# Loading the first batch of an attention kernel in token halves, with values sorted on TensorE

## The chip, the cores and the metric

The kernel runs on one core of a Trainium2 chip. The metric is device time in microseconds (us). Kernels of one set of experiments were timed on one chip, in rounds with runs of the kernel before on it, and are compared with those. The sets ran on different chips, on which the kernel before had medians of 236.9 to 237.4 us. Each run was checked for a slower state of the chip; none showed it.

## The reference

Four batches of 768 tokens with 8 heads of 64. Tokens attend in chunks of 32 to their chunk, 16 tokens to its left, 8 to its right and 8 memory tokens. The result, 512 wide, passes a layer to 2048 wide with a snake activation and a layer back to 512.

```python
for c in range(S // 32):                       # attention by chunks
    k_full = concat([mem_k, k[l_start:r_end]])
    a = softmax(q_c @ k_full.T / sqrt(64))
    out[c] = a @ concat([mem_v, v[l_start:r_end]])
h = x @ w_in                                   # x: 3072 x 512
s = sin(alpha * h)
g = h + s * s / (alpha + 1e-9)
return g @ w_out
```

## The kernel before

Batches run one behind the other. Of each, 8 blocks of 96 queries go through attention; then 16 tiles of the first layer (L1), with the second layer of the batch before it streamed between as filler. The change touches the opening, where batch 0 has nothing to hide behind. A piece is the k or q of two heads. Its heads are copied side by side (paired, tile pr), turned by six matmuls on TensorE (transposed, tile tt) and copied out of PSUM, the memory that matmuls write to, into kTi or qT (evicted). Filler matmuls (tile z) work on zeros and only keep TensorE busy. In the views PE is TensorE, DVE is VectorE, ACT is ScalarE and POOL is GpSimd, which also issues most of the loads (DMA).

```python
def spin(n):                        # filler matmuls on zeros
    z = smp.tile([P, 512], F32, name="z", tag="sm")
    for _ in range(n):
        nc.tensor.matmul(z[:], zeros[:, 0:P], zeros[:])
# ... 8 loads: k and q of two heads each, 128 partitions x 6 tokens
for hp in range(1, HP):
    load_qk_pair(0, hp, *kq)
# ... values: 2 loads a block, one token per descriptor
for j in range(NJ):
    load_v(0, j)
nc.sync.dma_start(alpha_sb[:], moe_alpha.rearrange("(ft p) -> p ft", p=P))
# ... a piece: pair two heads, transpose 6 x 128, evict
for n in range(2 * HP):
    (t_k if n % 2 == 0 else t_q)(prs[n], n // 2)
    spin(2)
# ... then, per block: scores and exponentials (sc, pt), values
# (ot, rinv, x_blk), transposes back (xtp, xT)
xT = burst(0, stream, (), 2)
# ... L1: u = sin, s = square, gT = h + s / alpha; the string says
# which engine squares each tile (A ScalarE, D VectorE, P GpSimd)
sq = ("ADADADAAADADADAA" if i == 0 else "ADAAPDADADAPADAD")[ft]
if 1 <= ft:
    stream.take(3 if last else 2)   # second-layer matmuls as filler
```

The softmax here doesn't subtract the row's maximum and nothing guards it: scores larger than these inputs give would overflow.

## Time and profile before

| | before |
|---|---|
| time, median of its first 3 runs | 237.71 us (237.04 to 239.23) |
| profiled span, mean granted clock | 234.8 us, 1.000 |
| first exponential | 17.06 us |
| last copy to xT (attention of batch 0 done) | 29.26 us |
| first sine (L1 of batch 0 begins) | 30.65 us |
| last gT of batch 0 | 55.09 us |
| first sine of batch 3 to the end | 51.12 us |

Times of events are counted from the start of the profiled span. The page, the chain and the groups are shown in the prediction.

### The profile page before, as it was taken

Reading aid. Unit: us, or ns where it says so; the run is one execution under the profiler, and the core shown is the slowest. Engines: PE = TensorE matmul, PEld = TensorE weight load, DVE = VectorE, ACT = ScalarE, POOL = GpSimd, SP = SyncE. Lnnn points to the kernel's source line nnn. Section 1 sums busy time; section 2 is a strip of 40 time slices with the busy share of each in tenths; the row PEclk is TensorE's granted clock in tenths of the full one; section 3 lists DMA queues with packets and bytes.
Section 4 is the critical chain, followed back from the end, with each engine's and each line's share of the span. In section 5 each row is a group of like instructions: output and inputs, shape, how many; then the busy total and the mean of one; then the engine's idle time right before and its main releaser. Section 6 shows DMA issues by size and latency. Waiting matters only on the chain.

```text
span 234.8 us, 4467 instructions
## 1 busy us (share of the span) xinstructions
PE 217.1 (92%) x1759; PEld 122.3 (52%) x1785; DVE 160.8 (69%) x287; ACT 153.8 (66%) x237; POOL 72.1 (31%) x96
## 2 busy tenths in 40 slices
PE   7588799979989999998999999998999999899994
PEld 2355565545545556664455556564555555453453
DVE  3596969999338877988557598978466358875110
ACT  3489679984794397899664787779564676880000
POOL 7899855214832115139120115120000020010000
PEclk9999999999999999999999999999999999999999
DMA  7999999999999910019999101001111110101122
GB/s 78 160 141 82 141 187 204 206 207 157 142 218 160 153 48 3 0 46 133 181 150 113 47 0 45 3 0 45 47 45 47 46 45 3 45 0 45 59 78 89
DMA packets 53852, 21.11 MB, mean 90 GB/s; under 512 B 36296, under 2 KB 50888, under 8 KB 53832
## 3 DMA queue, kind: packets, MB, share of 16 engines
q0 software_dynamic: 47616, 14.40, 72.4%
q1 hardware_dynamic: 6216, 6.43, 9.4%
q8 instruction: 14, 0.23, 0.4%
q14 instruction: 6, 0.05, 0.1%
HBM read 28.91 MB, written 6.29 MB: 150 GB/s over the span
## 4 chain that ended last, share of the span: by engine, by line
PE 60%; DVE 15%; ACT 11%; issue 7%; DMA 3%; POOL 2%; POOLq 1%; DVEq 0%; ACTq 0%
PE o L398 29%; PE hT L341 19%; DVE gT L370 6%; ACT pt L275 4%; ACT u L353 3%; DMA q_bf<-in_q_dram 3%; PE ot L288 3%; DVE s L362 3%; PE sc L266 3%; ACT s L356 2%; PE ot L306 2%; DVE x_blk L293 2%; PE o L387 1%; PE tt_a L257 1%; PE tt_a L242 1%
## 5 line engine op out<-in xcount | busy, mean ns | idle before, releaser
L398 PE MATMUL o<-w_out_sb,gT 128*128 128x512 bf16 x343 | 93.1, 380 | 2.0 <-issue 0.5
L341 PE MATMUL hT<-xT,w_in_sb 128*128 128x384 bf16 x488 | 87.3, 326 | 3.8 <-DVE gT L370 3.4
L370 DVE SCALAR_TENSOR_TENSOR gT<-s,inv_alpha,hT 128x768 bf16<-128x768 f32 x61 | 60.8, 1012 | 21.6 <-ACT s L356 13.7
L353 ACT ACTIVATE u<-hT,alpha_sb 128x768 f32<-128x768 f32 x61 | 54.7, 898 | 25.5 <-PE hT L341 24.4
L341 PEld LDWEIGHTS <-w_in_sb 128*128 128x128 bf16 x512 | 49.3, 98 | 38.5 <-issue 4.7
L275 ACT ACTIVATE pt<-sc,biasm 128x256 bf16<-128x256 f32 x96 | 37.6, 493 | 12.5 <-PE sc L266 12.4
L398 PEld LDWEIGHTS <-gT 128*128 128x128 bf16 x368 | 31.9, 98 | 26.1 <-DVE gT L370 1.2
L358 POOL TENSOR_TENSOR s<-u 128x768 f32<-128x768 f32 x6 | 8.8, 1466 | 71.6 <-ACT u L353 61.3
L356 ACT ACTIVATE s<-u 128x768 f32<-128x768 f32 x34 | 28.7, 843 | 1.1
L362 DVE TENSOR_TENSOR s<-u 128x768 f32<-128x768 f32 x24 | 24.9, 1036 | 0.6 <-ACT u L353 0.5
L293 DVE TENSOR_TENSOR x_blk<-ot,rinv 96x512 bf16<-96x512 f32 x32 | 22.0, 686 | 1.1
L226 POOL COPY pr<-q_bf 128x768 bf16<-128x768 bf16 x12 | 10.1, 839 | 38.6 <-PE tt_a L242 23.7
L292 DVE RECIPROCAL rinv<-ot 96x8 f32<-96x8 f32 x32 | 6.5, 202 | 20.1 <-PE ot L288 19.6
L407 ACT COPY o_sb<-o 128x512 f32<-128x512 f32 x11 | 6.4, 585 | 20.0 <-PE o L398 20.0
L405 DVE COPY o_sb<-o 128x512 f32<-128x512 f32 x12 | 8.2, 687 | 15.4 <-PE o L398 15.1
L288 PEld LDWEIGHTS <-pt 128*128 128x128 bf16 x256 | 11.9, 98 | 7.3 <-issue 2.3
L171 PE MATMUL z<-zeros 128*128 128x512 bf16 x36 | 13.2, 451 | 1.3 <-DVE zeros L165 1.3
L288 PE MATMUL ot<-vw,pt 128*128 128x65 bf16 x256 | 13.0, 193 | 0.9 <-ACT pt L275 0.6
L266 PEld LDWEIGHTS <-kTi 64*128 64x128 bf16 x256 | 7.0, 94 | 13.2 <-issue 6.7
L266 PE MATMUL sc<-qT,kTi 64*128 64x96 bf16 x256 | 11.4, 205 | 2.1 <-ACT pt L275 1.2
L306 PEld LDWEIGHTS <-x_blk 96*128 96x128 bf16 x128 | 8.4, 97 | 6.6 <-DVE x_blk L293 1.6
L226 POOL COPY pr<-k_bf 128x768 bf16<-128x768 bf16 x8 | 6.6, 826 | 11.2 <-PE tt_a L257 5.8
(66 smaller groups left out, 180.6 us busy)
## 6 DMA issues: line engine op xcount, KB each, us to landing
out_dram<-o_sb SPq DMA_DIRECT2D x23, 256.0 KB, 2.5
k_bf<-in_k_dram POOLq DMA_DIRECT2D x3, 768.0 KB, 9.1
q_bf<-in_q_dram POOLq DMA_DIRECT2D x3, 768.0 KB, 12.9
vw<-in_v_dram POOLq DMA_DIRECT2D x6, 384.0 KB, 17.7
w_in_sb<-in_moe_w_in_dram POOLq DMA_DIRECT2D x8, 256.0 KB, 9.0
w_out_sb<-in_moe_w_out_dram POOLq DMA_DIRECT2D x4, 512.0 KB, 18.5
k_bf<-in_k_dram POOLq DMA_DIRECT2D x4, 192.0 KB, 6.1
q_bf<-in_q_dram POOLq DMA_DIRECT2D x4, 192.0 KB, 6.7
```

The lines of the kernel that those rows point to most:

```text
L171: nc.tensor.matmul(z[:], zeros[:, 0:P], zeros[:])
L226: (eng or nc.gpsimd.tensor_copy)(pr[:].rearrange("p r e d -> p e r d"), src[:, 2 * hp:2 * hp + 2])
L266: nc.tensor.matmul(sc[:, e, QW * hp:QW * hp + QW], kTi[64 * e:64 * e + 64, hp, 104 * j:104 * j + P], qT[64 * e:64 * e + 64, hp, QW * j:QW ...
L275: nc.scalar.activation(pt[:, 0:H * QW].rearrange("p (g e c) -> p e g c", g=4, e=2)[:, :, :, 32 * m:32 * m + 32], sc[:, :, 0:4 * QW].rearra ...
L288: nc.tensor.matmul(otv[:, h // 4, h % 4, :], pt[:, QW * h:QW * h + P], vws[b % 2][:, h, j, 0:D + 1])
L293: nc.vector.tensor_tensor(out=x_blk[:].rearrange("p (g e) d -> p g e d", g=2), in0=otv[0:QW, :, :, 0:D], in1=rv.unsqueeze(3).to_broadcast( ...
L341: nc.tensor.matmul(hts[hf][:, 0:HALF], w_in_sb[:, kt, P * ft:P * ft + P], xT[:, kt, HALF * hf:HALF * hf + HALF], start=(kt == 0), stop=(kt ...
L353: nc.scalar.activation(u[:], hT[:, :, 0:HALF], ACTF.Sin, scale=alpha_sb[:, ft:ft + 1])
L356: nc.scalar.activation(s2[:], u[:], ACTF.Square)
L362: nc.vector.tensor_tensor(out=s2[:], in0=u[:], in1=u[:], op=ALU.mult)
L370: nc.vector.scalar_tensor_tensor(out=gv, in0=s2[:], scalar=inv_alpha[:, ft:ft + 1], in1=hT[:, :, 0:HALF], op0=ALU.mult, op1=ALU.add)
L398: nc.tensor.matmul(o[:], gT[:, ft, P * s:P * s + P], w_out_sb[:, ft, :], start=(ft == 0), stop=(ft == FT - 1),)
```

## The change

The intent is an earlier start and more overlap in the opening. The first k and q loads bring what the first four query blocks need (576 of the 768 tokens of k, 384 of q). Those blocks may begin while the second halves still load, and one hand-written order mixes the rest in. Values of blocks 0 to 3 are loaded two tokens per descriptor, which halves the number of descriptors. They arrive in the wrong rows, so 4 matmuls with a selection matrix put each pair of blocks in order. A few smaller edits ride along: fewer fillers after the pieces, larger weight loads, half of the first L1 tile begun early, another square string, and fewer second-layer matmuls per tile in the last batch.

```diff
-    for hp in range(1, HP):
-        load_qk_pair(0, hp, *kq)
+    load_qk_part(0, k, kq[0], 0, 0, 96)      # 4 heads, partitions 0:96
+    load_qk_part(0, q, kq[1], 0, 0, 64)
+    load_qk_part(0, k, kq[0], 4, 0, 96)
+    load_qk_part(0, q, kq[1], 4, 0, 64)
...
-    for j in range(NJ):
-        load_v(0, j)
+    for j in range(4):
+        load_v_pairs(j)                      # 2 tokens per descriptor
+    load_qk_part(0, k, kq[0], 0, 96, P)      # second halves
... (three more second halves, then load_v for blocks 4 to 7)
+    def put_v(i, eng):                       # sort two blocks
+        ps = big.tile([P, 2, 512], F32, name="vp", tag="big")
+        for e in range(2):
+            for c in range(2):
+                nc.tensor.matmul(ps[:, c], sel[64 * c:64 * c + 60, e],
+                    v2[64 * c:64 * c + 60, i, :, D * e:D * e + D],
+                    start=(e == 0), stop=(e == 1))
+        eng(vws[0][...], ps[...])
+        put_memv_part(2 * i, 2)
...
-        spin(2)                              # after each first piece
+        spin(1)
...
-    xT = burst(0, stream, (), 2)
+    for word in (  # Q scores, V sort, P values, X xT, R pair, T transpose,
+                   # Z filler, W/N loads, M memory values, E early L1 half
+        "M0 Q0 Z1 Q1 Z1 V0 Q2 P0 V1 Q3 Z1 X0 R8 R9 P1 T8 R10 T9 R11 W0 W1 X1 Z1 T10 T11 R12 R13 Z1 T12 "
+        "R14 T13 R15 W2 W3 W4 Z1 T14 T15 N0 Z1 Q4 P2 Z1 Q5 Q6 P3 X2 P4 Q7 X3 P5 X4 P6 X5 P7 E0 X6 X7"
+    ).split():
+        at(word[0], int(word[1:]))
...
-            sq = ("ADADADAAADADADAA" if i == 0 else ...)[ft]
+            sq = ("ADADAAPADPADPAPA" if i == 0 else ...)[ft]
-                stream.take(3 if last else 2)
+                stream.take(2)
```

## The prediction

> **What bounds the kernel now.** I read, in this order, the page, the chain that ended last (part 4, then in order of time), the groups of instructions of the opening stretch, VectorE's timeline, and the landing of each early load. The change rewrites only the opening (batch 0), so the first question is what sets the end of the opening.
>
> From the page, busy tenths of 40 slices of 5.87 us:
>
> ```profile
> PE   7588799979989999998999999998999999899994
> ...
> DVE  3596969999338877988557598978466358875110
> ACT  3489679984794397899664787779564676880000
> POOL 7899855214832115139120115120000020010000
> ...
> DMA  7999999999999910019999101001111110101122
> ```
>
> TensorE is the bound of the whole (92%), but it is full only from about slice 5 on. In slices 0 to 4 (0 to 29 us) much of its work is filler matmuls on zeros (36 of them, 13.2 us in the groups). So what counts is when the first layer of batch 0 starts; all that follows is a chain behind it.
>
> The chain in order of time, 0 to 60 us (start, length, what):
>
> ```profile
> 5.66 6.97 DMA q_bf<-in_q_dram
> 12.64 0.02 issue
> 12.66 0.46 DVE pr L226
> 13.12 0.61 DVE kTi L243
> ...
> 17.06 5.59 ACT pt L275 x15
> ...
> 24.47 0.69 DVE x_blk L293
> 25.16 0.27 DVE xT L309
> 25.42 0.13 DVE rinv L292
> ...
> 28.90 0.37 DVE xT L309
> 29.27 0.04 issue
> 29.32 1.31 PE hT L341 x7
> 30.63 0.02 issue
> 30.65 0.91 ACT u L353
> ```
>
> It reads as three legs. To 12.7 us the loads of k and q; to 17.06 the pairing, transposing and evicting; then exponentials and, from about 22 us, VectorE alone, which repeats reciprocal, scaling and copy at 1.1 us a block (0.13 + 0.69 + 0.27). The first sine starts at 30.65 us. The reader should note who has room: in 5.5 to 29.3 us the stretch view gives VectorE 17.8 us busy of 23.8, so only 6.0 idle, and most of that is early: 4.7 us waiting for k and q to land, 1.9 for the first values' matmuls.
>
> The groups that price the change, 5.5 to 29.3 us:
>
> ```profile
> L293 DVE TENSOR_TENSOR x_blk<-ot,rinv 96x512 bf16<-96x512 f32 x8 | 5.5, 686 | 0.3
> L243 DVE COPY kTi<-tt_b 128x672 bf16<-128x672 bf16 x3 | 2.6, 851 | 0.8 <-PE tt_b L242 0.8
> L226 DVE COPY pr<-k_bf 128x768 bf16<-128x768 bf16 x4 | 1.9, 464 | 4.2 <-DMA k_bf<-in_k_dram 4.2
> ```
>
> [...]the early loads share one stream: issued 0.7 us apart (1.32, 2.26, 3.52, 4.24, 4.95, 5.66, 6.37, 7.08), they land one after another at 5.6, 7.7, 8.9, 10.7, 11.7, 12.7, 13.7 and 14.6 us. [...]672 bf16 elements out of PSUM take 851 ns, 768 within SBUF as little as 359. This prices the sorted values, which come out of PSUM in fp32. [...]a value load whose issue takes 0.75 us elsewhere took 1.37 us at 16.38 us, beside the 8x4096 copy of VectorE (16.24 to 17.47), and the pair copies spread from 359 to 623 ns while GpSimd issued loads. So I price new pair copies at 0.42 us, not at their best.
>
> **The change, part by part.**
>
> Loads. First k is now 96 rows of 4 heads (1.5 of the old loads), first q 64 rows of 4 heads (1 load), then the same again: five old loads in place of eight. Interpolated in the landings above: 6.6, 8.3, 10.7 and 11.7 us. The last needed before the first scores comes 2.9 us sooner than 14.6.
>
> Values. The first four blocks are 4 loads in place of 8, so GpSimd saves 4 issues of 0.7 us, and w_in is 5 loads in place of 8; the weights come some 5 us sooner. No wait on w_in stands in the chain of before, so this alone buys nothing.
>
> To the first exponential. VectorE must, in its own order after 10.7 us: pair k (0.42), two small memory copies (0.22 + 0.20), evict the second k piece, pair, evict, pair a q, evict. A k piece of 480 columns scales from 851 ns to about 0.57, with one 48-column copy 0.13: 0.70. Sum 0.42 + 0.42 + 0.70 + 0.42 + 0.70 + 0.42 + 0.70 = 3.8, so 14.5; the last q piece and the score matmuls make the first exponential 15.1. That is 2 us before 17.06.
>
> From there VectorE owes, in pitch rather than length: reciprocal 0.2; the cast of memory values, moved here from ScalarE (2048 elements, estimate 1.2); memory rows into the values 1.3; one eviction of sorted values (1024 fp32 from PSUM; 512 take 0.67 in the output copy, so 1.2); eight second-half pair copies, 8 x 0.42 = 3.4; four second-half k evictions of 192 and 48 columns, 4 x 0.4 = 1.6; eight blocks at 1.1 = 8.8. Sum 17.7, so 32.2 if it never waits. Before, the same stretch held the memory rows, a reciprocal and the blocks: about 10.5 us in 12.2. Against the whole stretch the change adds about 5.9 us of VectorE work to an engine that had 6.0 idle, and some 4 us of that idle (the wait for the first load's successors, the tail) cannot be filled.
>
> Waits inside: the build's order shows the copy of memory rows behind ScalarE's eviction of the second pair of blocks (about 0.9), block 2's values behind the last transposes and scores (about 1.1), and the first sorted values behind their matmuls (0.5). Some hide; I take 1.8. So the last xT copy ends at about 34.0, against 29.26. The first half of tile 0 of the first layer is then already done, so the sine follows after 4 matmuls (0.65) instead of 8: 34.8 against 30.65, a **loss of 4.1 us**.
>
> First layer of batch 0. Squares go from 10 ScalarE, 6 VectorE to 8, 4 and 4 on GpSimd. From 30.65 to 55.10 VectorE is busy 21.7 and ScalarE 22.4 of 24.45; TensorE needs 128 x 0.163 = 20.9. ScalarE saves 2 x 0.75 = 1.5, VectorE 2 x 0.9 = 1.8; but a GpSimd square takes 1.47 us and holds its PSUM tile longer, and three such tiles rotate. I take **0.9 us gained** of 1.5.
>
> Last batch. Two filler matmuls a tile instead of three spread what is left of the layer before over more tiles. TensorE idles 0.88, 0.27, 0.38 us and less around 204 to 214 us, where the filler has run out. I take **0.8 gained**.
>
> Sum: +4.1 - 0.9 - 0.8 = +2.4 us. My waits are hand-made and the order looks tuned, so I shade the loss to 1.3: 237.7 + 1.3 = 239.0.
>
> **Rivals.** First, the loads are the whole story: the start moves by 2 to 3 us and the rest hides in ScalarE's and TensorE's room; then about 234. For it: the chain's first leg is a load (6.97 us). Against it: VectorE's 1.1 us cadence from 22 us on, with no idle to take the extra copies. Second, VectorE waits more than I think, since half-pieces, values and blocks all pass it in one fixed order, and the transposes share two PSUM slots; xT then ends at 36 and the time is 242. Third, VectorE's pair copies run at 0.36 [...], and waits hide: xT at 32, time 236.5. A TensorE bound does not arise: the added transposes and the 8 sorting matmuls take under 5 us of time in which it now spins on zeros.
>
> **Range and chances.** From 236 (third rival with both gains in full) to 242 (second): I give 235.5 to 242.3. 2% is 4.75 us. Faster than 233.0 would need the first rival at its best: 0.04. Slower than 242.5 needs the second and no gains: 0.09. Same: 0.87.
>
> **What would show it.** First exponential near 15 us; VectorE almost without idle from 14 us to the last xT copy, which ends at 32 to 36; first sine near 34.8; pair copies of 64 rows still about 0.4 us; sorted-value copy about 1.2; first layer about 23.5 us from its first sine to its last gT; less TensorE idle in the last first layer. It is wrong if the first sine comes at or before 31 us, which means VectorE had room that I did not see, or if weights turn out to be waited for.

## More of the kernel before

One view more is needed here. It gives the busy time of each engine over one stretch, with the number of instructions in brackets, the granted TensorE clock and the busy share of the data-transfer engines. The stretch is from the end of the last k eviction to the last xT, in the kernel before:

```profile
core 0: us, PE busy (x) PEld busy (x) DVE busy (x) ACT busy (x) POOL busy (x), PEclk, DMA share, GB/s
16.24:29.26 13.02, 10.74 (x173) 6.84 (x173) 10.47 (x27) 10.66 (x26) 12.48 (x17) 1.00 1.24 108
```

VectorE (DVE) is busy for 10.47 of 13.02 us, so it waits 2.5 us. The clock is full (1.00).

## The result, and the profile after

The changed kernel took 249.23 us (median of 4 runs, 247.83 to 249.85), against 237.38 us (237.04 to 239.23) for the kernel before in the same rounds. The ratio is 1.0474, with a 95% interval of 1.0403 to 1.0545: slower. A ratio here is the mean time of one kernel's fast runs over that of the other's of the same rounds, so it is not quite the ratio of the medians.

| us | before | after | difference |
|---|---|---|---|
| first exponential | 17.06 | 18.12 | +1.06 |
| last xT | 29.26 | 42.63 | +13.37 |
| first sine, batch 0 | 30.65 | 43.53 | +12.88 |
| L1 of batch 0, first sine to last gT | 24.44 | 25.85 | +1.41 |
| last gT of batch 0 to first sine of batch 3 | 128.57 | 128.13 | -0.44 |
| first sine of batch 3 to the end | 51.12 | 50.06 | -1.06 |
| profiled span | 234.78 | 247.57 | +12.79 |

The whole loss lies before the first sine. Part 2 of the page of the changed kernel, in 40 slices of 6.19 us:

```profile
PE   5497798997899899999899999999999999999994
DVE  4375849779892687889865769898756468867101
PEclk9655556999999999999999999999999999999999
```

TensorE (PE) has holes in its first slices (4 in the second, 7 in the fourth and fifth), and its granted clock is half (5) from 7.4 to 41.6 us; before, it was full from 6.4 us on. The same stretch as above, last first-half k eviction to last xT, now reads:

```profile
16.90:42.63 25.73, 21.34 (x232) 13.27 (x230) 17.85 (x48) 14.01 (x31) 15.63 (x18) 0.52 1.28 159
```

VectorE has 17.85 us of work, where the prediction had 17.7, but it takes 25.73 us over it. It waits 7.9 us where the prediction gave 1.8. The view of waits for VectorE in this stretch names them (what waited, for what: total, times, longest):

```profile
DVE rinv L368 <- PE ot L364: 3.4, 3, 1.7
DVE vw L332 <- PE vp L327: 1.4, 1, 1.4
DVE kTi L299 <- PE tt_a L296: 1.2, 3, 0.5
DVE vw L160 <- ACT vw L332: 1.1, 1, 1.1
```

The second and fourth are the sorting: VectorE waits for the sorting matmuls, and later behind ScalarE's eviction of the second pair. The first is the output of the values, late because TensorE is late. The chain that ended last, in order of time, shows why (start, length, what):

```profile
3.41 8.19 DMA k_bf<-in_k_dram
11.73 0.35 DVE pr L255
...
12.27 0.59 PE z L184
12.85 0.43 PE tt_b L314 x6
13.28 0.54 PE z L184
13.82 0.48 PE tt_b L296 x6
...
19.53 0.98 PE vp L327 x4
20.54 1.24 DVE vw L332
21.80 0.43 DVE vw L160
...
22.37 0.60 PE ot L364 x8
22.97 0.99 PE vp L327 x4
23.98 1.02 ACT vw L332
25.02 0.42 DVE vw L160
```

The second load of first-half k lands at 11.6 us (issued at 3.41, 8.19 us), 0.9 later than predicted. From 12.3 to 20.5 us the chain is TensorE alone, a filler (z) in turn with a group of six transposes, and from 17.6 us with scores and sorting. Before, the chain of that time was a load, then the last piece on VectorE, TensorE and ScalarE, then exponentials. Then follows a relay: sorting, eviction, memory rows, values, sorting again. Each engine waits for the one before it.

### The profile page after: what moved, and what is told of

Same layout as the page of the kernel before. It is cut to its first block, busy times and chain, and to the rows that moved or that the text cites. A ratio compares the mean times of both kernels' runs of the same rounds, so it can differ in the third digit from the quotient of the medians.

```text
span 247.6 us, 4604 instructions
## 1 busy us (share of the span) xinstructions
PE 227.9 (92%) x1830; PEld 128.2 (52%) x1830; DVE 166.1 (67%) x307; ACT 153.0 (62%) x240; POOL 71.6 (29%) x91
## 4 chain that ended last, share of the span: by engine, by line
PE 67%; DVE 11%; ACT 8%; issue 7%; DMA 3%; POOL 2%; POOLq 1%; DVEq 0%; ACTq 0%
PE o L483 28%; PE hT L420 20%; DVE gT L455 5%; PE ot L364 4%; PE sc L342 4%; DMA k_bf<-in_k_dram 3%; ACT u L438 3%; PE z L184 3%; DVE s L447 2%; ACT pt L351 2%; POOL s L443 2%; PE ot L382 2%; PE o L472 1%; ACT s L441 1%; PE tt_a L286 1%
## 5 line engine op out<-in xcount | busy, mean ns | idle before, releaser
L483 PE MATMUL o<-w_out_sb,gT 128*128 128x512 bf16 x368 | 99.0, 380 | 0.6 <-DVE gT L455 0.4
L443 POOL TENSOR_TENSOR s<-u 128x768 f32<-128x768 f32 x10 | 14.7, 1470 | 91.1 <-ACT u L438 80.8
L441 ACT ACTIVATE s<-u 128x768 f32<-128x768 f32 x32 | 27.0, 844 | 1.0
L364 PEld LDWEIGHTS <-pt 128*128 128x128 bf16 x256 | 13.3, 106 | 7.7 <-issue 3.6
L364 PE MATMUL ot<-vw,pt 128*128 128x65 bf16 x256 | 14.7, 206 | 2.0 <-DVE vw L160 1.5
L342 PEld LDWEIGHTS <-kTi 64*128 64x128 bf16 x256 | 7.9, 103 | 14.2 <-issue 7.5
L342 PE MATMUL sc<-qT,kTi 64*128 64x96 bf16 x256 | 12.4, 222 | 1.3 <-DVE gT L455 0.6
L382 PEld LDWEIGHTS <-x_blk 96*128 96x128 bf16 x128 | 9.4, 104 | 6.8 <-DVE x_blk L369 1.0
L385 DVE COPY xT<-ot 128x384 bf16<-128x384 bf16 x24 | 8.3, 346 | 2.0 <-PE ot L382 2.0
```

The costliest lines, as they stand in the source:

```text
L342: nc.tensor.matmul(sc[:, e, QW * hp:QW * hp + QW], kTi[64 * e:64 * e + 64, hp, 104 * j:104 * j + P], qT[64 * e:64 * e + 64, hp, QW * j:QW ...
L364: nc.tensor.matmul(otv[:, h // 4, h % 4, :], pt[:, QW * h:QW * h + P], vws[b % 2][:, h, j, 0:D + 1])
L441: nc.scalar.activation(s2[:], u[:], ACTF.Square)
L443: nc.gpsimd.tensor_tensor(out=s2[:], in0=u[:], in1=u[:], op=ALU.mult)
L483: nc.tensor.matmul(o[:], gT[:, ft, P * s:P * s + P], w_out_sb[:, ft, :], start=(ft == 0), stop=(ft == FT - 1),)
```

## The experiments

Three suspects stood after the first look. **Theory A**: the clock fell to half because TensorE was left idle early, and everything on it became slow. **Theory B**: TensorE's own queue carries too much that need not be there (fillers, sorting) at a time when it is on the chain. **Theory C**: the fixed order of half pieces, values and blocks makes engines wait, whatever the clock. Next to these stood the late load and the square string. The expectations use other letters: their C is the clock (A here), their O and W are the order and the waits (C here), their F is the fillers (B here). "First sine" below is that of batch 0, and all of its times are of single profiles. Gains between variants of the changed kernel are differences of medians, some of them between chips.

| kernel | median us | ratio to before (95% interval) | first sine |
|---|---|---|---|
| before | 236.9 to 237.4 | 1 | 30.65 |
| changed | 249.23 | 1.0474 (1.0403 to 1.0545) | 43.53 |
| aft_warm | 247.19 | 1.0434 (1.0353 to 1.0515) | 41.66 |
| aft_warm_all | 249.59 | 1.0522 (1.0459 to 1.0585) | 43.29 |
| aft_no_fill | 246.42 | 1.0410 (1.0344 to 1.0476) | 39.99 |
| bef_no_fill | 238.22 | 1.0039 (0.9982 to 1.0096) | 31.76 |
| aft_halves | 246.73 | 1.0400 (1.0348 to 1.0453) | 40.24 |
| bef_v_pairs | 240.34 | 1.0138 (1.0099 to 1.0178) | 34.45 |
| bef_sq | 243.87 | 1.0283 (1.0217 to 1.0349) | 32.07 |
| aft_old_sq | 248.45 | 1.0467 (1.0414 to 1.0521) | 43.08 |
| bef_take2 | 235.60 | 0.9930 (0.9889 to 0.9972) | 30.71 |
| bef_alpha_take2 | 236.29 | 0.9971 (0.9938 to 1.0004) | 31.47 |
| aft_alpha | 247.80 | 1.0446 (1.0395 to 1.0496) | 42.44 |
| aft_pv_early | 248.54 | 1.0484 (1.0442 to 1.0526) | 43.04 |
| aft_t_first | 247.13 | 1.0409 (1.0344 to 1.0474) | 38.92 |
| aft_two_pools | 246.59 | 1.0406 (1.0364 to 1.0448) | 40.50 |
| aft_strip | 241.45 | 1.0207 (1.0152 to 1.0261) | 36.70 |
| aft_strip_act | 241.88 | 1.0217 (1.0157 to 1.0277) | 37.43 |
| aft_strip_warm | 243.89 | 1.0305 (1.0265 to 1.0346) | 39.05 |
| aft_strip_t_first | 240.12 | 1.0142 (1.0097 to 1.0186) | 34.56 |

All gave a correct result. Names with aft_ start from the changed kernel, those with bef_ from the kernel before.

### The clock: more fillers

```diff
 aft_warm
+    spin(8)
     for n in range(8):
         piece0(n)
-        spin(1)
+        spin(12 if n == 0 else 2)
 aft_warm_all: the same, and every Z1 of the order becomes Z2, Z3 ahead of P0
```

> The changed kernel with more filler matmuls before the first scores (8 before the first piece, 12 after it, 2 after each other piece, where it had 0, 1, 1). Theory C (clock): the granted TensorE clock fell to 0.5 at 7.4 us because TensorE stood idle for most of the window before, and that is most of the unforeseen loss. Then the clock stays 1.0 at least up to about 17 us, and if it holds after that the first sine moves from 43.5 to about 37 us and the time from 249.2 to about 243. Theory O (order): the opening is bound by VectorE and by the fixed order of the pieces and their waits; then the clock hardly matters and the first sine stays above 41 us, the time above 246.

> As aft_warm, and with two fillers in place of one at each later place of the opening, and three more before block 0's values. If aft_warm loses the clock again between 17 and 40 us, this one keeps it. Theory C: clock 1.0 throughout, first sine at 36 to 38 us, time 242 to 244. Theory O: no better than 246. If the clock is at 1.0 in both, this one is 0 to 1.5 us slower than aft_warm by the fillers alone.

With aft_warm the clock stayed full from 6.9 to 20.6 us, then went to and fro until 41.1. The first sine came 1.9 us sooner and the median fell by 2.0 us; the intervals of the two ratios overlap. With still more fillers (aft_warm_all) the clock held to 27.6 us, and all of the gain was lost again: first sine 43.29. So theory A gives at most a part, as far as fillers can test it: a longer full clock did not bring a shorter opening. The cleanest reading is from the first exponential to the first sine, where aft_warm has the order and the fillers of the changed kernel (226 matmuls and transposes in both) and 9.8 us less of half clock: 24.58 us in place of 25.41 (one profile each).

### Fewer fillers

```diff
 aft_no_fill
     for n in range(8):
         piece0(n)
-        spin(1)
... and every Z1 is taken out of the order
 bef_no_fill
         (t_k if n % 2 == 0 else t_q)(prs[n], n // 2)
-        spin(2)
```

> The changed kernel without any filler matmul after the first ten. The last two runs showed that holding the clock gained only 2 us and more fillers lost it again. Theory F: with TensorE at half clock each filler costs 0.43 us, and some 16 of them stand in TensorE's own order between pieces on the path; without them the first sine moves from 43.5 to about 39.5 and the time to about 245.5, though the clock stays low at least as long. Theory W (waits of VectorE on landings and on the fixed order alone): no change beyond 1 us, time 248.5 to 249.5. Theory C (clock): worse than 249.

> The kernel before without the two fillers after each of its eight pieces. Theory C: with the fillers gone the clock falls to 0.5 in the opening here too, and the first sine comes some 2 to 5 us later than 30.65 (time 239.5 to 242.5). Theory O: fillers are dead weight, the first sine stays at 30.7 or comes a little sooner, time 237 to 238.

Without fillers the changed kernel gained 2.8 us (intervals overlap; first sine 3.5 us sooner, first exponential at 16.05 in place of 18.12), although its transposes still took 0.50 us per six, as at half clock. In the kernel before, removal cost 1.2 us against the 237.05 us of its rounds, which its interval does not tell from zero; the clock was half from 9.1 to 22.7 us there. So the same fillers that were harmless before are a cost in the changed kernel. This speaks for theory B.

### The sorting

```diff
 aft_halves
-        load_v_pairs(j)
+        load_v(j, 16 if j == 0 else 0)     # plain loads for blocks 0 to 3 too
... V0 and V1 are taken out of the order; memory rows of all blocks at M0
 bef_v_pairs: the kernel before, with the paired loads and put_v
+            if b == 0 and s in (1, 3):
+                put_v(s // 2, (nc.vector.tensor_copy, nc.scalar.copy)[s // 2])
```

> The changed kernel with the values of the first four blocks loaded as before, token by token, and no sorting matmuls or evictions; the halves stay. If the sorting is the costly part (8 matmuls of 512 columns at half clock, two evictions of 1.2 and 1.0 us, waits of 1.5 and 1.1 us on them), the first sine comes 4 to 5 us sooner, time about 245. If the halves are, at most 1.5 us, time 247.7 or more, since the values' waits hide behind the second halves.

> The kernel before with only the values of the first four blocks loaded in pairs of tokens and sorted by TensorE, one eviction by VectorE, one by ScalarE. If sorting alone costs what it seems to (two evictions of 1.2 and 1.0 us on engines of the path, and the wait for them), the first sine comes 1.5 to 3 us after 30.65 and the time is 239 to 241. If it hides in the room that the kernel before has, the time stays at 237.4.

The changed kernel without sorting took 2.5 us less (intervals overlap); the kernel before with sorting took 3.1 us more, with an interval clear of 1, its first sine 3.8 us later. The two fit each other. The clock does not make the difference: six runs of the kernel before in the same rounds had a mean clock of 0.991 to 0.993, like bef_v_pairs (0.985 to 0.993), and a median of 237.2 us. In bef_v_pairs the waits were the same relay as above: VectorE 1.5 us for ScalarE's eviction, TensorE 1.7 us for the memory rows. Sorting is a cost on the path by itself, whatever the halves do.

### The square string

```diff
 bef_sq
-            sq = ("ADADADAAADADADAA" if i == 0 else "ADAAPDADADAPADAD")[ft]
+            sq = ("ADADAAPADPADPAPA" if i == 0 else "ADAAPDADADAPADAD")[ft]
 aft_old_sq: the reverse edit in the changed kernel
```

> The kernel before with only the new sequence of squares for batch 0 (8 on ScalarE, 4 on VectorE, 4 on GpSimd). My prediction said 0.9 us gained from the first sine to the last gT; the traces show 24.44 before and 25.85 after, but the changed kernel has other loads at that time. If GpSimd squares are themselves the cause: about 1.4 us slower, some 238.8, with a square of VectorE of about 2 us beside one of GpSimd. If not: 236.5 to 237.5.

> The changed kernel with the old sequence of squares for batch 0. In the trace after, the first layer of batch 0 takes 25.85 us from first sine to last gT against 24.44 before; in the run with the new squares on the old kernel 31.1, where the squares stood in GpSimd's queue behind loads. If the new squares cost by themselves: 24.4 here and the time 1.4 us less, about 247.8. If they save, as I predicted (0.9): about 250.1.

With the old string, L1 of batch 0 in the changed kernel took 24.36 us in place of 25.85; the time fell by 0.8 us, which is within noise. The traces are clearer than the times: L1 of batch 0 takes 25.83 to 25.85 us in all nine traces of the changed kernel and its variants with the new string, and 24.36 to 24.43 in the five with the old one. In the kernel before, the new string alone cost 6.8 us (2.8%): L1 took 31.1 us in place of 24.4. The timeline of GpSimd in bef_sq shows why (start, length, line, what, and in brackets the idle time ahead of it and what ended it):

```profile
41.33 0.78 POOL L145 DMA_DIRECT2D vw<-in_v_dram  x1 [2.39 <-DMA k_bf<-in_k_dram]
45.26 0.83 POOL L148 DMA_DIRECT2D vw<-in_v_dram  x1 [3.15 <-DMA q_bf<-in_q_dram]
46.11 1.48 POOL L358 TENSOR_TENSOR s<-u 128x768 f32<-128x768 f32 x1
```

The first square on GpSimd stands in its queue behind load issues, and these wait for earlier loads to land. VectorE waited 6.5 us for GpSimd's squares there. In the changed kernel the loads are fewer and earlier, and the waits for those squares are only 2.0 us. The string came with that kernel, and still did not pay in it. Its timelines show one square of each engine side by side:

```profile
56.54 2.19 DVE L447 TENSOR_TENSOR s<-u 128x768 f32<-128x768 f32 x1
56.45 1.47 POOL L443 TENSOR_TENSOR s<-u 128x768 f32<-128x768 f32 x1 [1.93 <-ACT u L438]
```

The VectorE square, begun just after the one of GpSimd, takes 2.19 us where 0.95 is usual. All nine traces with the new string have such a pair, the five with the old one none.

### The last batch

```diff
 bef_take2
-                stream.take(3 if last else 2)
+                stream.take(2)
```

> The kernel before with two filler steps a tile in the last first layer instead of three, nothing else. In the trace after, first sine of the last batch to the end is 50.06 us against 51.12. If this edit is the cause: 1.0 us faster, 236.0 to 236.4 beside 237.1. If the difference came from elsewhere: within 0.3.

The last batch took 50.04 us in place of 51.12, and the time was 235.60 us: 0.7% faster than before, over 5 rounds, with an interval clear of 1. The last batch takes 50.04 to 50.15 us in all 16 traces with this edit and 51.10 to 51.12 in the four without. Of the 1.6 us between the medians, some may be the clock: all six runs had a mean clock of 0.998 or more, and the six runs of the kernel before that had it in these rounds have a median of 236.47, 0.9 us above 235.60. This part of the change is good, and it is the fastest version.

### The load of alpha

```diff
 aft_alpha
-        nc.sync.dma_start(alpha_sb[:], moe_alpha.rearrange(...))
+        nc.gpsimd.dma_start(alpha_sb[:], moe_alpha.rearrange(...))  # queue behind the values
... and the reciprocal of alpha moves behind the order
 bef_alpha_take2: bef_take2 with the same edit
```

> The changed kernel with the same load of alpha moved behind the value loads. If alpha's small packets made the second k pieces land at 11.6 us and not at the predicted 10.7, they land near 10.5, the first exponential comes about 1 us before 18.12 and the time is about 248. If not, landings and time stay (11.6 us; 249).

> The kernel before with two filler matmuls a tile in the last batch (alone: 235.6 us) and the load of alpha, whose 2048 packets of 4 bytes share the load stream with the first k and q, moved behind the value loads. If the small packets delay the first k and q, the first sine comes 1 to 2 us before 30.65 and the time is about 234. If they only fill gaps, it stays at 235.6.

These loads go alike in kernels that differ otherwise. The second first-half k is paired at 11.65 to 11.79 us in eight of the nine traces of the changed kernel and its variants that load alpha early, and at 12.24 in the ninth; in the five that load it late (aft_alpha and the stripped kernels below) it is paired at 9.91 to 10.46. So in the eight, the early load of alpha's 8 KB goes with a delay of 1.2 to 1.9 us. The groups of pair copies from 5 to 16 us, first in the changed kernel, then in aft_alpha, show the wait:

```profile
L255 DVE COPY pr<-k_bf 96x768 bf16<-96x768 bf16 x4 | 1.3, 354 | 5.9 <-DMA k_bf<-in_k_dram 5.6 <-PE tt_b L314 0.2
```

```profile
L255 DVE COPY pr<-k_bf 96x768 bf16<-96x768 bf16 x4 | 1.3, 354 | 3.7 <-PE tt_b L314 1.9 <-DMA k_bf<-in_k_dram 1.7 <-ACT pr L255 0.2
```

The wait for the load falls from 5.6 to 1.7 us, nearly half of it turned into one for TensorE, and the first exponential comes at 16.85. The time falls by 1.4 us, with overlapping intervals. In the kernel before, the same edit gained nothing (236.29 against 235.60, k and q landing no sooner). The traces show the small packets beside the loads of k and q in both kernels. The queue of alpha and the memory tokens has 2,616 packets in the first 20 us, and 552 in aft_alpha, where alpha goes with the values. From 6.3 to 7.0 us of the kernel before it moved 1,042 packets and the queue of k and q 47, with 47 GB/s for all queues; from 7 to 8 us of the changed kernel 975 and 108, with 82 GB/s. Why the 2,048 packets of 4 bytes delay the halves and not the eight whole loads was not settled; alpha's load is issued at 2.62 us in both kernels.

### The order of the queues, and the PSUM tiles

All three start from aft_no_fill.

```diff
 aft_pv_early: values of blocks 2 and 3 ahead of the later transposes
-  ... W0 W1 X1 T10 T11 R12 R13 T12 R14 T13 R15 ... N0 Q4 P2 Q5 Q6 P3 X2 P4 ...
+  ... W0 W1 X1 P2 T10 T11 R12 R13 X2 T12 R14 T13 P3 R15 ... X3 N0 Q4 Q5 P4 ...
 aft_t_first: all second halves ahead of values and blocks
+  Q0 Q1 R8 R9 T8 R10 T9 R11 W0 W1 T10 T11 R12 R13 T12 R14 T13 R15 W2 W3 W4 T14 T15
+  M0 V0 V1 N0 Q2 P0 Q3 P1 X0 Q4 P2 X1 Q5 P3 X2 Q6 P4 X3 Q7 P5 X4 P6 X5 P7 X6 E0 X7
 aft_two_pools: second-half transposes use the large PSUM tiles in turn with the small
-    state["pools"] = 1
+    state["pools"] = 2
```

> The changed kernel without fillers (246.4 us, first sine at 39.99), with the values of blocks 2 and 3 and their output copies moved ahead of the later transposes and scores. If the fixed order of the queues is what makes VectorE wait, the first sine comes at about 38 us and the time is about 244.5. If the waits come from the half clock or from the work itself, both stay (40.0 us; 246.4).

> The changed kernel without fillers (246.4 us, first sine 39.99) in another order: all second halves are paired and transposed right after the scores of blocks 0 and 1, then values and blocks follow without interruption. If the mixing of half pieces, values and blocks in one fixed order makes the waits, they fall and the first sine comes at 37 to 38, time about 244.5. If the work itself and the half clock make them, it stays near 40 and 246.4.

> The changed kernel without fillers (246.4 us, first sine 39.99), with the transposes of the second halves alternating between the small and the large PSUM tiles in place of the two small ones alone. If the two small tiles hold the transposes back (ScalarE waits 4.9 us in all for them), the first sine comes 1 to 2 us sooner. If not, no change; later if they now hold up the scores.

The first was a miss: 2.1 us slower than aft_no_fill. The second is unclear: one run of 244.65 us, the profiled one, and three near 247.2. The third changed nothing (246.59), so the two small tiles are not what holds the transposes back. With sorting in, no order tried helped.

### Taking the costs out together

```diff
 aft_strip = aft_no_fill + aft_halves + aft_old_sq + aft_alpha
 aft_strip_act
-    h1_eng = [dv] * 8
+    h1_eng = [dv, ac] * 4                  # second-half q pairs on ScalarE
 aft_strip_warm: fillers put back as in aft_warm (one Z1 of the order left out)
 aft_strip_t_first: aft_strip in the order of aft_t_first, without V0 and V1
```

> The changed kernel with the four costs found so far taken out together: no fillers after the first ten, plain value loads without sorting, the old square string, alpha loaded late. Alone they gave 2.8, 2.5, 0.8 and 1.4 us. If they are separate costs they add: 249.2 - 7.5 = 241.7 us, first sine near 35, which leaves only the predicted VectorE work of the halves. If they overlap (the same wait is bought twice), it stays at 244 to 245.5.

> The same with the pair copies of the four second q pieces on ScalarE in place of VectorE (4 x 0.36 us off VectorE). If VectorE's work sets the pace, the first sine comes 1 to 1.5 us sooner than in the run beside it. If the chain of waits between the engines sets it, it comes no sooner, or later, as ScalarE takes 0.84 us for such a copy.

The four gains seen alone are 2.8, 2.5, 0.8 and 1.4 us, together 7.5, so 241.7 was expected if they are separate. 241.45 was measured. **They are not the same wait bought twice**: that would have given 244 us or more. The intervals of the single edits each overlap with that of the changed kernel, while that of aft_strip is far from it, so this is the firmest support for the four costs as a group. How exactly they add is within noise. By the ratios to before, the single gains are 0.6, 0.7, 0.1 and 0.3% (some 4.1 us together) and the joint one 2.7% (6.3 us); by the profiled spans they are 9.0 us together and 7.8 us jointly. Moving four pair copies off VectorE made it no faster (241.88), so VectorE's amount of work alone does not set the pace there. That its waits do fits this, but was not shown, as such a copy takes 0.83 us on ScalarE and 0.36 on VectorE.

> The stripped kernel (241.45 us, first sine 36.70, clock half from 8.9 to 36.2) with more fillers in the opening, 36 in place of 10 before the first exponential and the changed kernel's seven after it, to hold the full clock. If the half clock costs time of its own there, the first sine comes at about 35.5 and the time is about 240. If what the fillers take is as much as the clock gives, the time stays at 241.5 or rises towards 243.

> The stripped kernel with all second halves transposed before the first values and blocks. With sorting and fillers this order's profile came 1.1 us sooner at the first sine, its timed runs no sooner. If the order matters here, the first sine comes about 1 us before 36.70 and the time is 240.5. If not, 241.5.

(The text for aft_strip_warm counts 36 fillers; there are 44 before the first exponential.) Putting fillers back cost 2.4 us (the intervals do not overlap), although the clock was then full to 21.7 us. Here theory A, in the form "buy the clock with fillers", is refuted. The other order, on the other hand, gained 1.3 us in the median, its first sine 2.1 us sooner; the intervals still touch. The same stretch (from the last first-half k eviction to the last xT) and VectorE's waits in aft_strip_t_first:

```profile
14.40:33.66 19.26, 12.69 (x206) 9.96 (x207) 15.91 (x44) 12.60 (x30) 18.25 (x20) 1.00 1.17 124
```

```profile
DVE rinv L368 <- PE ot L364: 1.3, 3, 0.7
DVE kTi L299 <- PE tt_a L296: 1.3, 4, 0.3
```

Busy 15.91 of 19.26 us: waits of 3.4 us in place of 7.9. The clock column reads 1.00 only because its record begins at 27.6 us in this run; six transposes still took 0.50 us up to 22 us, as at half clock. Its four timed runs also hint at what the clock is worth by itself. The two with mean clock 0.943 took 240.73 and 241.05 us, the one with 0.957 took 239.5. That is some 7 us less of half clock for about 1.4 us (an estimate from 0.014 x 2 x 240). Three runs are too few to call it shown, and a record that begins late, as that of the fourth run does, reads as too high a mean clock.

## Why the prediction was wrong

**The direction of the first step was right, its size was not.** The prediction said that the opening would lose, because VectorE gets more work than the earlier loads give back. The first sine came 12.9 us later, not 4.1. The step that failed is "Waits inside ... I take 1.8": with them its working ended at a last xT of 34.0 us, where 42.63 was measured. In the terms of its own sum (start of the leg, VectorE's work, waits) it had 14.5 + 17.7 + 1.8; the trace has 16.90 + 17.85 + 7.9. So 6.1 of the 8.6 us are waits, and 2.4 are a late first leg. The rejection of a bound on TensorE failed with it: "A TensorE bound does not arise: the added transposes and the 8 sorting matmuls take under 5 us of time in which it now spins on zeros." TensorE was busy for 21.34 of the 25.73 us, at a mean clock of 0.52, where it had been busy for 10.74 of 13.02 at full clock.

1. **Loads.** Predicted 6.6, 8.3, 10.7, 11.7; the pair copies of these pieces began at 6.60, 9.31, 11.73 and 12.77. Interpolating between landings of the kernel before left out alpha's packets, which delay the second k here. With alpha late, it is paired at 9.91. Cost: 1.4 us in time (intervals overlap).
2. **First exponential.** Predicted 15.1, measured 18.12. Fillers (16.05 without) and alpha (16.85 without) make up the difference: without both, and without sorting, it comes at 14.48. The leg itself was sound on VectorE: predicted 4.4 us from the second k to the exponential, 4.5 in aft_strip (from 10.01). What the sum left out was TensorE, which stood on the chain from 12.3 us on.
3. **VectorE's work.** Predicted 17.7, measured 17.85. (The 10.5 us that the prediction sets beside it for the kernel before are those of 16.24 to 29.26; from 17.06 on it is 9.65 of 12.20.) The single prices held as well, or made up for each other: the sorted eviction 1.23 (1.2), the cast of memory values 1.22 (1.2), the pair copies 0.36 (0.42), a second-half k eviction 0.49 (0.40).
4. **Waits.** Predicted 1.8, measured 7.9, of which sorting is shown as a cause (clear of noise in bef_v_pairs), fillers nearly so (2.8 us less without them with overlapping intervals; clear of noise where aft_strip_warm puts them back in greater number), and the order is a likely one (its gain of 1.3 us has intervals that touch). The prediction did count these hand-overs, one by one, but as small and partly hidden. What it missed, as the chain shows, is that they stand behind one another. Sorting, eviction, memory rows and values pass through three engines, and TensorE's place in that relay comes after its fillers. Here spinning on zeros was free only while TensorE had time to spare; the prediction took the 13.2 us of fillers in the kernel before as time to be used, but of the 27 fillers that follow the first ten, the changed kernel keeps 16, now on the chain.
5. **The clock.** The prediction did not mention it. In two traces the times between its changes are multiples of some 3.4 us: in the changed kernel it is full from 4.0 to 7.4 us and half from there to 41.6, ten times that; in aft_warm (read from stretches of 2 us) it falls at about 20.6, 27.4 and 37.6 and is full again at 24.0, 34.2 and 41.1. The changed kernel left TensorE idle from 4.94 to 7.02 and from 7.76 to 10.20 us, where the kernel before had no hole longer than 1.49. Of the 3.4 us before its clock fell, TensorE was idle for 2.1. With more fillers there (aft_warm) it stayed full to 20.6 us, and without its fillers the kernel before had it half from 9.1 to 22.7. How much idle time brings it down was not shown, nor why it then stayed half for 34 us: from 12 to 18 us TensorE was busy for 5.78 of 6.00 us, at 0.50. A filler takes 0.61 us at half clock in the changed kernel and 0.38 to 0.39 at full clock in the kernel before; the first ten of the changed kernel start 0.43 us apart up to 3.8 us and 0.21 from 4.1 us, where its clock record begins, at full. A set of six transposes of 64 rows takes 0.50 us at half clock in the changed kernel, and 0.34 to 0.35 at full clock in aft_warm. How much of the 12.9 us this is by itself was not settled, because every way to hold the clock cost fillers. Two hints lie apart. At the rate of aft_warm after the first exponential (0.83 us for 9.8 us of half clock) the 34 us of half clock would be worth some 3 us. The kernel before took a median of 238.30 us in its 6 timed runs with a mean clock of 0.986 and of 236.64 in the 19 with 0.998 or more, 1.7 us for some 6.6 us of half clock; at that rate it would be 8 to 9 us. Both are estimates, and the second is only a correlation, as what delays TensorE may also lower its clock. So the half clock stays a rival for part of the loss, also of what aft_strip keeps.
6. **L1 of batch 0.** Predicted 0.9 gained, measured 1.4 lost. The price of a GpSimd square (1.47) was right, that of a ScalarE square (0.84, reckoned with as 0.75) nearly so, but VectorE waited 2.0 us for them, and a VectorE square beside one of GpSimd took 2.19 us in place of 0.95. In the pair shown above the VectorE square ends 0.81 us after the one of GpSimd. Why it takes longer there was not shown.
7. **Last batch.** Predicted 0.8 gained, measured 1.1 in the profile, and 1.6 in the medians of bef_take2's rounds (237.19 against 235.60), of which 0.9 is left at equal clock. The direction was right and the size nearly so.
8. **Shading.** The sum was +2.4, and it was shaded to +1.3 because "the order looks tuned". The order was probably part of the loss. The range ended at 242.3 on the same ground, with the rival of longer waits put at 242.

aft_strip_t_first has its first sine at 34.56 us, where the prediction had 34.8. That is partly chance: without sorting VectorE has 15.91 us of work there and not 17.7, and it still waits 3.4 us and not 1.8. It is still 4.5 us slower than the kernel before with the same last-batch edit (240.12 against 235.60): splitting pieces in halves makes 16 pair copies of 8 and 16 groups of transposes of 8, and its first exponential comes only 2 us sooner (15.04 against 17.06). What of the 4.5 us is the halves and what the half clock was not taken further apart.

## What to carry to other kernels

When work is added to an opening, write down one engine's order at a time and ask of every hand-over which engine must finish what before it; a sum of busy times gives a floor, and the waits between three engines can add nearly half as much again (7.9 beside 17.85 us here). In these runs filler matmuls were free only off the chain: when a change makes TensorE part of the chain, take them out first and look at the clock afterwards. When parts of a change ride together, time each alone; here one line (0.7% faster) was worth keeping, and everything around it cost 5%.
